# Attention inside a fused attention and MLP kernel: plain float32 products in two halves of the tensor engine, in place of products of split float32r parts

## The chip, the core and the metric

One core of one Trainium2 chip runs the whole kernel. The metric is the device time of one execution in microseconds (us), from the profiler's first to last instruction or from the timed runs. A core has a tensor engine (TensorE; PE in the rows, its weight loads PEld), a vector engine (DVE), a scalar engine (ACT), GpSimd (POOL) and a sync engine (SP), which here issues DMAs. Each works through its own list of instructions in order; semaphores tie the lists together. TensorE writes to PSUM, 8 banks of 2 KB per partition; the other engines copy from there to SBUF.

## What is computed

The kernel chains three parts. The change is in the first:

```python
batch, n_heads, seq, head_dim = (4, 12, 448, 64)
q_n, k_n = rmsnorm(q, g_q), rmsnorm(k, g_k)
scores = (1 / sqrt(head_dim)) * q_n @ k_n.T
attn = exp(scores - max(scores)); attn = attn / sum(attn)
attn_out = attn @ v                       # float32
x = attn_out as [1792 tokens, 768]
x = top-1 mixture of 8 experts (768 -> 1024 -> 768), gated
return two-layer MLP (768 -> 2048 -> 768)
```

All inputs and outputs are float32.

## The kernel before

The attention works on 24 pairs of heads (a, b of one batch). The 448 tokens of a head are three columns of 128 and a tail of 64; the two tails share one column, so a pair has seven columns a0 a1 a2 t b0 b1 b2. The schedule is written out by hand: seven slots a pair, one column a slot. In a slot TensorE does four transposes of probabilities (turn_p, L296), the scores of a column (scores, L276) and a part of the product with v (mix, L341 and L342); transposes of q and k (L229, L246) and the product that brings the result back to rows of tokens (back, L366 to L370) come between. DVE takes the row maxima (L281), ACT the exponentials (L287). Scores run ahead: turn_p is five slots behind them and mix seven.

The products of the attention use float32r, which TensorE takes in one pass, with every float32 operand split into two float32r parts, a high and a low one. Both parts of a query, 64 dimensions each, lie below each other on the 128 partitions, as weights; keys come as two tensors kh and kl. So one score column of a head is two products of 448 columns with all 128 rows of the array (all four part products). The tail column takes four, with weights padded by zeros (qm). The product with v is of the same kind: weights are the parts of v side by side (64 + 64 columns), and the probabilities are split after their transpose, into ph by ACT (L322) and pl by DVE (L330).

The splits are made by ACT (high parts: L199, L209, L248, L322) and by DVE or GpSimd (low parts: L204, L214, L253, L330). The normalized keys are doubled side by side by a DMA or a copy (kn). GpSimd also does the 1/rms by Newton's method and parts of the sums.

The product back (L366 to L370) multiplies by a matrix comb, [identity; identity] and 8 columns of the gate's weights, in plain float32. A plain float32 product is one instruction in the program and two in the trace, each with its own weights. The tails of the two heads go to the two halves of one output (L366 to partitions 0 to 63, L367 to 64 to 127), with 64 columns of weights each; these are the only products of the kernel before that stand side by side in the array.

In the first pairs some extra transposes of the identity (fill, L269) keep TensorE busy. After each batch of six pairs the routing of its tokens runs in small steps between the slots. The end of the last pair is written out by hand, together with the first transposes for the experts (L1027); the expert products start at L982. What follows does not change.

Of the kernel before, what the change touches and what calls it, by code (L numbers as in the profile page):

```python
# [8 lines left out]
F32 = mybir.dt.float32  # L9
# [7 lines left out]
E = 8  # L17
SLOTS = 1792
ND = 8
# [10 lines left out]


def attention(tc, ctx, q, k, v, const, ps, late, finish_half, tick, early):
# [8 lines left out]
    ident, identr, comb, gg = const["ident"], const["identr"], const["comb"], const["gg"]  # L41
    pool = lambda name, bufs: ctx.enter_context(tc.tile_pool(name=name, bufs=bufs))
    raw_p, spl_p, sm_p, tr_p, pp, phl, fix = (pool("raw", 2), pool("spl", 2), pool("sm", 2), pool("tr", 2), pool("pp", 2),
                                              pool("phl", 3), pool("fix", 1))
    NP = B * H // 2
    NR = 3
    qm, vm, pm = [], [], []

    def setup(*rs):
        for r in rs:  # L50
            qm.append(fix.tile([128, 2, 128], F32R, name=f"qm{r}"))
            vm.append(fix.tile([128, 2, 128], F32R, name=f"vm{r}"))
            pm.append(fix.tile([128, 576], F32, name=f"pm{r}"))
            nc.gpsimd.memset(qm[r].bitcast(F32), 0.0)
            nc.gpsimd.memset(vm[r].bitcast(F32), 0.0)
            nc.gpsimd.memset(pm[r], 0.0)
    st = [dict() for _ in range(NP)]

    # ---- per pair, before its scores
    def load(p, names):  # L60
        R = st[p]
        b, h = divmod(2 * p, H)
        for nm in names:
            src = dict(q=q, k=k, v=v)[nm]
            t = raw_p.tile([128, 8, D], F32, name="raw" + nm, tag="raw" + nm, bufs=3 if nm == "v" else 4)
            R[nm] = t[:, 0:7]
            nc.sync.dma_start(out=t.rearrange("p (i c) d -> p i (c d)", i=2)[:, :, 0:3 * D],
                              in_=src[b, h:h + 2, 0:384].rearrange("i (p c) d -> p i (c d)", c=3))
            nc.sync.dma_start(out=t[:, 3], in_=src[b, h:h + 2, 384:448])

    # 1/rms of the tokens of one or two pairs at a time
# [4 lines left out]
    fill = {0: 2, 2: 4, 4: 4, 14: 2, 16: 3}  # L76

    # what the vector engine takes from GpSimd, pair by pair, until GpSimd is ahead
    on_vector = dict(scale_k=(0, 1, 2), scale_q=(0, 2), q_low=(0,), v_low=(0,), sums=(0, 2, 3, 8), root=(0, 1))
# [4 lines left out]
    def squares(p, i):  # L84
        R, Z = st[p], sh[batch_of[p]]
        if i == 0:
            R["sq"] = raw_p.tile([128, 2, 7, D], F32, name="sq", tag="sq")
            if p == batch_of[p][0]:
                Z["ms"] = sm_p.tile([128, 2, 2, 7], F32, name="ms", tag="ms")[:, 0:len(batch_of[p])]
# [20 lines left out]
    def root(p, i=None):  # L110
        """1/rms by Newton's method, an instruction at a time; of a batch, or of k (i = 0) or q of a pair"""
# [6 lines left out]
        small = lambda name, dt=F32: sm_p.tile([128, 28], dt, name=name, tag=name)[:, 0:n]  # L118
# [33 lines left out]
        yv = y.rearrange("p (b a u o) -> p b a u o", a=2, u=7, o=1)  # L152
        rq = sm_p.tile([128, 2, 7, 1], F32, name="rq", tag="rq")[:, 0:len(bt)]
# [21 lines left out]

    def scale_k(p):
        R = st[p]
        R["kn"] = spl_p.tile([128, 7, 2, D], F32, name="kn", tag="kn")
        eng = engine("scale_k", p)
        eng.tensor_tensor(out=R["kn"][:, :, 0], in0=R["k"], in1=R["rk"].to_broadcast([128, 7, D]), op=ALU.mult)  # L180
        if p < 2:
            copy_k(p)
        elif p > 3:
            nc.sync.dma_start(out=R["kn"][:, :, 1], in_=R["kn"][:, :, 0])

    def copy_k(p):
        R = st[p]
        nc.vector.tensor_copy(out=R["kn"][:, :, 1], in_=R["kn"][:, :, 0])

    def scale_q(p):  # L190
        R = st[p]
        R["qn"] = raw_p.tile([128, 7, D], F32, name="qn", tag="qn")
        eng = engine("scale_q", p)
        eng.tensor_tensor(out=R["qn"], in0=R["q"], in1=R["rq"].to_broadcast([128, 7, D]), op=ALU.mult)

    def q_high(p):
        R = st[p]
        R["qs"] = spl_p.tile([128, 7, 2, D], F32R, name="qs", tag="qs", bufs=3)
        nc.scalar.activation(out=R["qs"][:, :, 0], in_=R["qn"], func=ACTF.Copy)  # L199

    def q_low(p):
        R = st[p]
        eng = engine("q_low", p)
        eng.tensor_tensor(out=R["qs"][:, :, 1], in0=R["qn"], in1=R["qs"][:, :, 0].bitcast(F32), op=ALU.subtract)  # L204

    def v_high(p):
        R = st[p]
        R["vs"] = spl_p.tile([128, 7, 2, D], F32R, name="vs", tag="vs", bufs=3)
        nc.scalar.activation(out=R["vs"][:, :, 0], in_=R["v"], func=ACTF.Copy)  # L209

    def v_low(p):
        R = st[p]
        eng = engine("v_low", p)
        eng.tensor_tensor(out=R["vs"][:, :, 1], in0=R["v"], in1=R["vs"][:, :, 0].bitcast(F32), op=ALU.subtract)  # L214

    def v_tail(p):
        t = st[p]["vs"][:, 3].rearrange("p a d -> p (a d)")
        for i in range(2):
            s = slice(64 * i, 64 * i + 64)
            nc.gpsimd.tensor_scalar(out=vm[p % NR][s, i], in0=t[s].bitcast(F32), scalar1=1.0, scalar2=1.0, op0=ALU.mult, op1=ALU.mult)  # L220

    def turn_q(p, i):
        R = st[p]
        if i == 0:
            R["Q"] = tr_p.tile([128, 6, 128], F32R, name="Q", tag="Q", bufs=3)
        us = (0, 1, 2, 3) if i == 0 else (4, 5, 6)
        t = ps.tile([128, 4, 128], F32R, name="tq", tag="pt" if p == 0 else "tq")
        for j, u in enumerate(us):
            nc.tensor.transpose(out=t[:, j], in_=R["qs"][:, u].rearrange("p a d -> p (a d)"), identity=identr)  # L229
        tf = t.bitcast(F32)  # L230
        nc.scalar.activation(out=R["Q"][:, 3 * i:3 * i + 3], in_=tf[:, 0:3], func=ACTF.Copy)
        if i == 0:
            m = qm[p % NR]
            nc.scalar.activation(out=m[:, 0, 0:64], in_=tf[:, 3, 0:64], func=ACTF.Copy)
            nc.scalar.activation(out=m[:, 1, 64:128], in_=tf[:, 3, 64:128], func=ACTF.Copy)

    def turn_k(p, i):
        R = st[p]
        if i == 0:
# [1406 lines left out]
```

## Time and profile before

| what | value |
|---|---|
| median of 3 timed runs | 1177.55 us (1176.89 to 1181.33) |
| span of the profiled execution (the only time given for it) | 1178.3 us |
| first score product of the attention | 16.6 us |
| last score product of the attention | 346.7 us |
| first product of the experts | 358.7 us |
| TensorE busy, whole span | 97% |
| mean granted clock of TensorE | 0.992 of full speed |

The attention takes the first 30% of the span. The span is 0.7 us above the median of the timed runs; sums below are made against the span. A share of busy time over the whole span says little on the attention; it is read from the stretches of its pairs.

### The profile page before, as it was taken

To read this page: it belongs to the slowest core of one execution; us is meant where nothing else is said; L and a number is where in the kernel's file an instruction comes from. 1 tells how busy PE (TensorE), PEld (TensorE's weight loads), DVE (VectorE), ACT (ScalarE), POOL (GpSimd) and SP (SyncE) were. 2 spreads that over 40 slices of the span, in tenths; PEclk is the share of its full clock that TensorE was granted. 3 is DMA by queue.
4 is the path that set the end of the run, shared out by engine and by line. 5 is a ranking of instruction groups with operands and counts; after the bars stand their busy time and mean duration, and the time that the engine had idled before them with its cause. 6 is when DMAs were issued, how large, how long until landed. Compare 5 with 4: busy or idle time off the path is not lost. (4 is left out here: it accounts for less than half of the span.)

```text
span 1178.3 us, 20906 instructions
## 1 busy us (share of the span) xinstructions
PE 1140.2 (97%) x7189; PEld 1009.1 (86%) x7189; DVE 879.5 (75%) x1709; ACT 732.5 (62%) x1494; POOL 409.0 (35%) x644
## 2 busy tenths in 40 slices
PE   6899999999998999999999999999999999999997
PEld 5778888888888998999999978888888888888996
DVE  7898988988977666888988978885644445444674
ACT  6889989888864566665556645553544345443664
POOL 5777676765421122255554444440200001000100
PEclk8999999999999999999999999999999999999999
DMA  4323323223036689899999923340200001000100
GB/s 113 79 64 93 113 63 106 69 64 93 17 95 186 196 283 293 264 325 284 280 301 296 297 78 107 108 129 19 108 1 1 1 14 68 1 1 1 54 1 28
DMA packets 145368, 138.25 MB, mean 117 GB/s; under 512 B 39903, under 2 KB 125919, under 8 KB 144741
## 3 DMA queue, kind: packets, MB, share of 16 engines
q1 hardware_dynamic: 141252, 120.30, 34.2%
q0 software_dynamic: 4000, 16.53, 4.0%
q8 instruction: 59, 0.97, 0.3%
q14 instruction: 57, 0.46, 0.1%
HBM read 117.26 MB, written 18.10 MB: 115 GB/s over the span
## 5 line engine op out<-in xcount | busy, mean ns | idle before, releaser
L974 DVE TENSOR_TENSOR l<-ld,h 128x768 fp32r<-128x768 f32 x159 | 151.6, 970 | 18.9 <-ACT h L969 16.3
L946 POOL TENSOR_SCALAR cva<-cva 128x384 f32<-128x384 f32 x64 | 110.3, 1724 | 144.1 <-ACT cva L945 143.8
L969 ACT ACTIVATE h<-ld 128x768 fp32r<-128x768 f32 x159 | 130.6, 840 | 9.9 <-PE hs L993 6.5
L1466 POOL DMA_INDIRECT out_dram<-ld,oidx x11 | 12.8, 1162 | 336.6 <-ACT ld L1463 212.9
L281 DVE TENSOR_REDUCE nb<-s 128x1 f32<-128x448 f32 x168 | 103.8, 618 | 22.1 <-PE s L276 20.8
L1418 ACT ACTIVATE u<-hp,half 128x512 f32<-128x512 f32 (+1 forms) x64 | 40.4, 631 | 110.2 <-PE hp L982 110.2
L330 DVE TENSOR_TENSOR pl<-pt,ph 128x448 fp32r<-128x448 f32 (+1 forms) x168 | 104.1, 620 | 4.8 <-ACT ph L322 4.7
L287 ACT ACTIVATE P<-s,nb 128x448 f32<-128x448 f32 x144 | 92.5, 642 | 22.4 <-DVE nb L281 21.7
L1425 DVE SCALAR_TENSOR_TENSOR w<-u 128x512 f32<-128x512 f32 (+1 forms) x64 | 39.9, 624 | 84.3 <-ACT u L1418 84.1
L322 ACT ACTIVATE ph<-pt 128x448 fp32r<-128x448 f32 (+1 forms) x168 | 93.4, 556 | 8.6 <-PE pt L296 7.2
L1190 ACT ACTIVATE rh<-hp 128x256 fp32r<-128x256 f32 x64 | 24.6, 384 | 107.3 <-PE hp L982 107.3
L982 PE MATMUL hp<-yh,h 128*128 128x512 f32 (+1 forms) x384 | 88.9, 368 | 2.2 <-DVEq L1369 2.2
L1016 PE MATMUL a<-l,gh 128*128 128x512 f32 x240 | 89.8, 404 | 0.0
L1016 PE MATMUL a<-h,gh 128*128 128x512 f32 x240 | 89.0, 400 | 0.0
L1016 PE MATMUL a<-h,gl 128*128 128x512 f32 x240 | 88.8, 400 | 0.0
L982 PE MATMUL hp<-yl,h 128*128 128x512 f32 (+1 forms) x384 | 87.8, 365 | 0.0
L1433 DVE TENSOR_TENSOR gl<-u,gh 128x512 fp32r<-128x512 f32 (+1 forms) x64 | 40.2, 628 | 63.6 <-ACT gh L1432 63.4
L982 PE MATMUL hp<-yh,l 128*128 128x512 f32 (+1 forms) x384 | 87.3, 363 | 0.0
L1432 ACT ACTIVATE gh<-u 128x512 fp32r<-128x512 f32 (+1 forms) x64 | 36.9, 576 | 80.8 <-PE a L1017 78.3
L296 PE MATMUL pt<-ident,P 128*128 128x128 f32 x504 | 82.4, 273 | 0.0
L982 PEld LDWEIGHTS hp<-yl,h 128*128 128x128 f32 x384 | 67.3, 190 | 11.4
L982 PEld LDWEIGHTS hp<-yh,l 128*128 128x128 f32 x384 | 66.8, 189 | 11.2
(342 smaller groups left out, 3452.8 us busy)
## 6 DMA issues: line engine op xcount, KB each, us to landing
ld<-in_moe_w_dram SPq DMA_DIRECT2D x160, 384.0 KB
raw<-in_moe_w_in_dram SPq DMA_DIRECT2D x32, 384.0 KB
ld<-in_moe_w_out_dram SPq DMA_DIRECT2D x26, 384.0 KB
rawk<-in_k_dram SPq DMA_DIRECT2D x24, 192.0 KB
rawq<-in_q_dram SPq DMA_DIRECT2D x24, 192.0 KB
rawv<-in_v_dram SPq DMA_DIRECT2D x24, 192.0 KB
xt_d<-x SPq DMA_DIRECT2D x4, 1152.0 KB
kn<-kn SPq DMA_DIRECT2D x20, 224.0 KB
```

Of the source, the lines that this page charges most:

```text
L281: nc.vector.tensor_reduce(out=R["nb"][:, u:u + 1], in_=R["s", u], op=ALU.max, axis=AX.X, negate=True)
L287: nc.scalar.activation(out=o, in_=R.pop(("s", u)), func=ACTF.Exp, bias=R["nb"][:, u:u + 1], accum_out=R["sum"][:, w:w + 1])
L296: nc.tensor.transpose(out=out, in_=src, identity=ident)
L322: nc.scalar.activation(out=R["ph", m], in_=t, func=ACTF.Copy)
L330: nc.vector.tensor_tensor(out=R["pl", m], in0=t, in1=R["ph", m].bitcast(F32), op=ALU.subtract)
L946: nc.gpsimd.tensor_scalar(out=R["a"], in0=R["a"], scalar1=2.0 ** -15, scalar2=122879.9921875, op0=ALU.max, op1=ALU.min)
L969: nc.scalar.activation(out=h, in_=src, func=ACTF.Copy)
L974: (engine or self.nc.vector).tensor_tensor(out=l, in0=src, in1=h.bitcast(F32), op=ALU.subtract)
L982: nc.tensor.matmul(out=t[:, 0:n], lhsT=w[:, k], rhs=x[:, k, 0:n], start=i == 0 and k == 0, stop=i == 2 and k == 5)
L1016: nc.tensor.matmul(out=a[j], lhsT=p[:, c], rhs=q[:, 0:512], start=first and i == 0, stop=last and i == 2)
L1418: nc.scalar.activation(out=u, in_=t[:, s], func=ACTF.Relu, scale=0.5, bias=half)
L1433: nc.vector.tensor_tensor(out=gl[:, 0:n], in0=u, in1=gh[:, 0:n].bitcast(F32), op=ALU.subtract)
```

## The change

The splits go. A score column of a head is one plain float32 product with the 64 dimensions of that head on 64 partitions: head a on partitions 0 to 63, head b on 64 to 127, so that the two heads use the upper and the lower half of the array's rows. The product with v puts head a on output partitions 0 to 63 and head b on 64 to 127 (64 columns of weights each). The tails' column uses a quarter of the array for each head.

A pair now has four units instead of seven slots, three columns with both heads and one of tails. A unit has eight transposes (five in the tails' unit), the scores of both heads into two PSUM banks, and the product with v. Head b's scores are made in two pieces of 64 and 384 columns, so that its tail keys come first. There is one row maximum for both heads (896 columns), two exponentials, and one plain copy for each head of the transposed probabilities (take_p, one by ACT, one by DVE). The schedule keeps its seven slots; units stand in the even ones, and the turning of q, of k and the product back have one even slot each. Keys are no longer doubled; q and k of four pairs stay in fixed tiles. PSUM: pt 2 banks, s 4, av 1, tq 1 (before 2 each). The fill transposes are gone, and the last pair's end is written anew.

```diff
     def scores(p, u):
         R = st[p]
-        t = ps.tile([128, S], F32, name="s", tag="s")
-        for _ in range(fill.get(7 * p + u, 0)):
-            nc.tensor.transpose(out=t[:, 0:128], in_=ident, identity=ident)
-        if u == 3:
-            ops = [(qm[p % NR][:, i], R[nm, i]) for i in range(2) for nm in ("kh", "kl")]
-        else:
-            i = u // 4
-            ops = [(R["Q"][:, u - i], R[nm, i]) for nm in ("kh", "kl")]
-        for j, (w, x) in enumerate(ops):
-            nc.tensor.matmul(out=t, lhsT=w, rhs=x, start=j == 0, stop=j == len(ops) - 1)
+        t = ps.tile([128, 2, 512], F32, name="s", tag="s", bufs=2)
+        for i, h in enumerate(halves2):
+            if u < 3:
+                o, w = t[:, i], R["Q"][h, 128 * u:128 * u + 128]
+            else:
+                o, w = t[h, 0], R["Q"][h, 384:S]
+            x = R["K"][h]
+            for d, n in ((0, S),) if i == 0 else ((384, 64), (0, 384)):
+                e = (d + 64 * i) % S
+                nc.tensor.matmul(out=o[:, e:e + n], lhsT=w, rhs=x[:, d:d + n], start=True, stop=True)
...
+    def take_p(p, m, i):
+        R = st[p]
...
+        o, t = R["PT", m][:, i, 0:S], R["pt", m][i][:, 0:S]
+        if i == 0:
+            nc.scalar.activation(out=o, in_=t, func=ACTF.Copy)
         else:
+            nc.vector.tensor_copy(out=o, in_=t)
 
     def mix(p, m):
         R = st[p]
-        for i in ((0,), (0,), (0,), (0, 1), (1,), (1,), (1,))[m]:
...
-            nc.tensor.matmul(out=R["av", i], lhsT=w, rhs=R["ph", m][:, c], start=first, stop=False)
-            nc.tensor.matmul(out=R["av", i], lhsT=w, rhs=R["pl", m][:, c], start=False, stop=last)
+        if m == 0:
+            R["av"] = ps.tile([128, S], F32, name="av", tag="av", bufs=1)
+        for i, h in enumerate(halves2):
+            if m < 3:
+                nc.tensor.matmul(out=R["av"][h], lhsT=R["v"][:, 4 * i + m], rhs=R["PT", m][:, i, 0:S], start=m == 0, stop=False)
+            else:
+
+                for d, n in ((64, 384), (0, 64)) if i == 0 else ((64, S),):
+                    e = (d - 64) % S
+                    nc.tensor.matmul(out=R["av"][h, e:e + n], lhsT=R["v"][h, 3], rhs=R["PT", m][h, 0, d:d + n], start=False, stop=i == 1 or d == 0)
...
+        t = ps.tile([128, 7, 72], F32, name="xo", tag="tq")
+        o = R["o"]
         for c in range(3):
...
+            nc.tensor.matmul(out=t[:, 2 * c:2 * c + 2], lhsT=o[:, 128 * c:128 * c + 128], rhs=comb[:, r], start=True, stop=True)
+        for i, h in enumerate(halves2):
+            nc.tensor.matmul(out=t[h, 6], lhsT=o[h, 384:S], rhs=comb[h, r, i], start=True, stop=True)
...
+    LAG = 5
+    for n in range(7 * NP):
+        t = n % 7
+        s = n // 7 * 4 + t // 2
+        if t % 2 == 0:
+            at(turn_p, s, LAG)
+            for f, a in onpe.get(n, ()):
+                f(*a)
+            at(scores, s, 0)
...
+            at(mix, s, LAG + 1)
+            at(expo, s, 1, 0)
+            at(take_p, s, LAG, 0)
+            at(take_p, s, LAG, 1)
...
+            if t == 6:
+                at(expo, s, 1, 1)
+            at(row_max, s, 0)
+        else:
+            at(expo, s, 1, 1)
```

TensorE in the kernel before, one slot in the middle of the attention (pt: transposed probabilities, s: scores, tk: transposed keys, av: the product with v):

```order
L296 MATMUL pt<-ident,pm_377 128x128
L296 MATMUL pt<-ident,P 128x128 x3
L276 MATMUL s<-kh,Q 128x448
L276 MATMUL s<-kl,Q 128x448
L246 MATMUL tk<-ident,kn 128x128 x4
L341 MATMUL av<-ph,vs 128x448
L342 MATMUL av<-pl,vs 128x448
```

Here all products use the whole array, and transposes, scores and the product with v follow each other in one form. TensorE in the changed kernel, one unit at the same place (xo: the product back; each row that is no transpose of pt is a float32 product):

```order
L247 MATMUL pt<-ident,pm_157 128x128
L247 MATMUL pt<-ident,P 128x128 x3
L247 MATMUL pt<-ident,pm_157 128x128
L247 MATMUL pt<-ident,P 128x128 x3
L314 MATMUL xo<-comb,osb 128x144 x3
L316 MATMUL xo<-comb,osb 64x72 x2
L223 MATMUL s<-K,Q 128x448
L223 MATMUL s<-K,Q 128x64
L223 MATMUL s<-K,Q 128x384
L288 MATMUL av<-pT,rawv 64x448 x2
```

Whole array (L247, L314), quarters (L316), row halves (L223) and column halves (L288) now follow each other inside every unit.

ACT in the kernel before, in the middle of the attention (sq: squares for the rms, osb: the copy of av out of PSUM):

```order
L287 ACTIVATE P,sum<-s,nb 128x448
L322 ACTIVATE ph<-pt 128x448
L94 ACTIVATE sq<-rawk 128x448
L287 ACTIVATE P,sum<-s,nb 128x448
L322 ACTIVATE ph<-pt 128x448
L94 ACTIVATE sq<-rawq 128x448
L350 ACTIVATE osb<-av 128x448
```

and in the changed kernel:

```order
L204 ACTIVATE K<-tq,gg 128x448
L239 ACTIVATE P,sum<-s,nb 128x448
L278 ACTIVATE pT<-pt 128x448
L298 ACTIVATE osb<-av 128x448
L239 ACTIVATE P,sum<-s,nb 128x448 x2
L278 ACTIVATE pT<-pt 128x448
```

An exponential (L239) now shares ACT with one copy for every two of them instead of one each, and the copies of q, v and the high parts are gone.

## Rows read from the trace of the kernel before

**Rows 1.** The page: busy time of each engine, share of the span, instructions.

```profile
PE 1140.2 (97%) x7189; PEld 1009.1 (86%) x7189; DVE 879.5 (75%) x1709; ACT 732.5 (62%) x1494; POOL 409.0 (35%) x644
```

**Rows 2.** Stretches from pair to pair: length; busy PE, PEld, DVE, ACT, POOL; clock; DMA.

```profile
16.60:28.40 11.80, 9.40 (x53) 6.42 (x51) 10.45 (x31) 9.35 (x27) 5.05 (x12) 0.90 0.55 125
...
88.10:101.00 12.90, 12.90 (x93) 11.52 (x92) 11.14 (x25) 12.51 (x33) 8.34 (x16) 1.00 0.42 106
88.10:170.00 81.90, 79.86 (x560) 69.81 (x558) 74.98 (x187) 74.64 (x194) 58.64 (x127) 1.00 0.33 89
```

**Rows 3.** Score products of the six whole columns of all pairs: durations, first and last start.

```profile
L276 PE MATMUL s<-kh,Q x144: 447/450/741, 16.6 to 346.7; 128*128 128x448 f32 x144
```

**Rows 4.** TensorE in order of time, one slot: start us, us, engine, line, what.

```profile
183.43 0.27 PE L296 MATMUL pt<-ident,pm 128*128 128x128 f32 x1
...
183.78 0.45 PE L276 MATMUL s<-kh,Q 128*128 128x448 f32 x1
184.07 0.36 PE L276 MATMUL s<-kl,Q 128*128 128x448 f32 x1
184.27 0.36 PE L341 MATMUL av<-ph,vs 128*128 128x448 f32 x1
184.68 0.38 PE L296 MATMUL pt<-ident,pm 128*128 128x128 f32 x2
```

**Rows 5.** Eight float32 passes of 128 columns, with 112 columns of weights.

```profile
340.10 1.04 PE L762 MATMUL ptab<-olg,ohi 128*112 128x128 f32 x8
340.89 0.45 PE L341 MATMUL av<-ph,vs 128*128 128x448 f32 x1
```

**Rows 6.** The tails' products side by side, last pair: weight loads, then products.

```profile
357.74 0.13 PEld L366 LDWEIGHTS xo<-comb,osb 128*64 128x64 f32 x1 [0.40 <-PE tp L1027]
357.77 0.13 PEld L367 LDWEIGHTS xo<-comb,osb 128*64 128x64 f32 x1
357.79 0.14 PEld L366 LDWEIGHTS xo<-comb,osb 128*64 128x64 f32 x1
357.83 0.14 PEld L367 LDWEIGHTS xo<-comb,osb 128*64 128x64 f32 x1
358.04 0.19 PEld L370 LDWEIGHTS xo<-comb,osb 128*128 128x128 f32 x1
...
357.85 0.23 PE L366 MATMUL xo<-comb,osb 128*64 128x72 f32 x1
357.89 0.23 PE L367 MATMUL xo<-comb,osb 128*64 128x72 f32 x1
```

**Rows 7.** TensorE before and after the tails' products of another pair.

```profile
185.43 0.37 PE L276 MATMUL s<-kl,Q 128*128 128x448 f32 x1
185.72 0.28 PE L366 MATMUL xo<-comb,osb 128*64 128x72 f32 x1
186.00 0.89 PE L370 MATMUL xo<-comb,osb 128*128 128x72 f32 x6
```

**Rows 8.** Groups of instructions, 0 to 400 us: busy us, mean ns | idle before.

```profile
L281 DVE TENSOR_REDUCE nb<-s 128x1 f32<-128x448 f32 x168 | 103.8, 618 | 22.1 <-PE s L276 20.8
L322 ACT ACTIVATE ph<-pt 128x448 fp32r<-128x448 f32 (+1 forms) x168 | 93.4, 556 | 8.6 <-PE pt L296 7.2
L287 ACT ACTIVATE P<-s,nb 128x448 f32<-128x448 f32 x144 | 92.5, 642 | 22.4 <-DVE nb L281 21.7
L287 ACT ACTIVATION_READ_ACCUMULATOR P<-s,nb 128x1 f32 x144 | 30.0, 209 | 0.0
```

**Rows 9.** The start of the first pair, in order of time.

```profile
11.33 1.13 DVE L194 TENSOR_TENSOR qn<-rawq,rq 128x448 f32<-128x448 f32 x1
...
16.64 0.74 PE L276 MATMUL s<-kh,Q 128*128 128x448 f32 x1
```

**Rows 10.** The end of the attention: last scores, first products of the experts.

```profile
346.70 0.45 PE L276 MATMUL s<-kh,Q 128*128 128x448 f32 x1
...
358.73 0.95 PE L982 MATMUL hp<-xh,e 128*128 128x256 f32 x6
```

More of the change, by code (lines that the diff above doesn't have):

```diff
@@ L206, in v_high @@
[L206 to L235, printed above, removed]
@@ new lines, in scale_k, with turn @@
+    def scale_k(p):
+        scaled(p, "kn", st[p]["k"], st[p]["rk"])
+    def scale_q(p):
+        scaled(p, "qn", st[p]["q"], st[p]["rq"])
+    def turn(p, x, name):
+        t = ps.tile([128, 512], F32, name="tq", tag="pt" if name == "Q" and p == 0 else "tq", bufs=2 if name == "Q" and p == 0 else 1)
+        for c in range(4):
+            nc.tensor.transpose(out=t[:, 128 * c:128 * c + 128], in_=x[:, 2 * c:2 * c + 2].rearrange("p i d -> p (i d)"), identity=ident)
+        st[p][name] = tr_p.tile([128, S], F32, name=name, tag=name)
+        return t[:, 0:S], st[p][name]
@@ L257, in scores, with turn_q, turn_k @@
+    def turn_q(p):
+        t, o = turn(p, st[p]["qn"], "Q")
+        nc.vector.tensor_copy(out=o, in_=t)
+    def turn_k(p):
+        t, o = turn(p, st[p]["kn"], "K")
+        nc.scalar.activation(out=o, in_=t, func=ACTF.Copy, scale=gg)
     def scores(p, u):
@@ L352, in invert, with mixed @@
+    def mixed(p):
+        R = st[p]
+        R["o"] = tr_p.tile([128, S], F32, name="osb", tag="osb")
+        nc.scalar.activation(out=R["o"], in_=R.pop("av"), func=ACTF.Copy)
     def invert(p):
@@ L393, in put @@
     def put(n, f, p, *a):
         m = place.get(p, {}).get(f.__name__, n)
-        sched.setdefault(m if type(m) is int else m[a[0]], []).append((f, (p,) + a))
+        if f is load and a == ("v",):
+            m = n
+        m = m if type(m) is int else m[a[0]]
+        (onpe if f in (turn_q, turn_k, back) and m >= 0 else sched).setdefault(m, []).append((f, (p,) + a))
     for bt in batches:
@@ L400, in attention @@
             y = z + 7 * (j - (len(bt) - 1))
-            put(y - 37, load, p, "kq")
+            put(y - 33, load, p, "kq")
             put(y - 29, squares, p, 0)
@@ L481, in begin @@
             else:
                 f(*a)
[L483 removed]
     begin()
[L485 to L502 removed]
+    N = 4 * NP
@@ L519 @@
+    turn_p(y, 3)
+    expo(z, 3, 0)
+    take(y, 3)
+    mix(y, 2)
+    turn_p(z, 0, "s")
+    mix(y, 3)
+    take(z, 0)
+    mixed(y)
+    turn_p(z, 1)
+    invert(z)
+    back(y)
+    take(z, 1)
+    mix(z, 0)
+    finish(y)
+    turn_p(z, 2, "s")
+    mix(z, 1)
+    take(z, 2)
+    turn_p(z, 3)
+    take(z, 3)
+    early(0)
+    mix(z, 2)
+    early(3)
+    mix(z, 3)
+    mixed(z)
+    early(1)
+    early(6)
+    early(4)
+    back(z)
+    finish(z)
+    early(2)
+    early(5)
 class Route:
@@ L1565, in late @@
                 else:
-                    for p in halves:
-                        nc.sync.dma_start(out=comb[p, :, 64:72], in_=wv)
+                    for i, p in enumerate(halves):
+                        nc.sync.dma_start(out=comb[p, :, i, 64:72], in_=wv[i])
                     route.load(moe_modality_id, moe_modality_bias)
```

336 lines of the change are left out of this document (121 added, 215 removed).

## The prediction

> **What bounds the kernel now.** I read the page first, then the stretches of single pairs, then TensorE in order of time. The page shows TensorE busy for 97% of the span [rows 1], which says where to look and not more, since ends of products are modelled. The stretches say it for the attention: a pair without routing takes 12.9 us, with TensorE busy for all of it, DVE for 11.1 and ACT for 12.5 at full granted clock, 1.00 or 2.4 GHz [rows 2]. So DVE and ACT have little room, but TensorE has none. Six pairs with one batch's routing take 81.9 us, 4.5 more than six times 12.9 [rows 2]. The order of time agrees: a slot of four transposes and four float32r products takes 1.25 us, from 183.43 to 184.68, and a product 0.20 (184.07 to 184.27) [rows 4]; the transposes are left with (1.25 - 4 x 0.205) / 4 = 0.11 each. Seven such slots are 8.75 us; turning q and k, the tails' extra products and the product back fill the 12.9.
>
> **Price of a float32 product.** The trace has no float32 product of 448 columns. Eight float32 passes of 128 columns take 0.79 us, 340.10 to 340.89, about 0.10 each [rows 5]; in the last pair a pass of 72 columns takes 0.06, from the weights' load at 357.79 (when the pass before it starts) to 357.85 [rows 6]. That is 0.77 to 0.83 ns a column, against 0.20/448 = 0.46 for float32r. I take 0.385 us for a pass of 448 and 0.77 for its two passes: one float32 product costs as much as almost four of float32r. The change has 16 such products a pair (four units, two heads, scores and v) in place of 32 of float32r, 32 x 0.205 = 6.6 us. Alone they would be 12.3 us; in pairs that run side by side 6.2. So on products TensorE gains next to nothing even if the halves overlap fully.
>
> **Do halves overlap?** Column halves do. The weights of L366 and L367 are loaded 0.03 us apart, the second passes' weights 0.04 apart, and the second passes start 0.04 apart, though a pass takes 0.06 [rows 6]: the two heads' passes alternate and run side by side. This carries the product with v. No product here has its rows in halves; for the scores the price lies between full overlap and none.
>
> **Price of changing the form.** From the last whole-array product at 185.43, which ends at 185.63, to the weights' load of the first half product at 185.72 pass 0.09 us in which nothing is issued [rows 7]. On the way back it is the same: the last half pass starts at 357.89 and ends 0.06 later, at 357.95; the next whole weights load at 358.04, 0.09 later [rows 6]. And the load, hidden otherwise, is now in the open: 0.055 us for 64 columns (357.74 to 357.79 [rows 6]) and about 0.11 for 128 (six passes from 186.00, each with its load, span 0.89 with the last one's 0.28 [rows 7], so 0.12 from one to the next, where 72 columns alone take 0.06). So a change costs 0.09 plus a load, and a unit has three: whole to rows, rows to columns, columns to whole; the tails of the product back add one a pair. The Trainium skill, page "TensorEngine Tiling (Array Packing)", section "Key Properties", says that a change of tiling mode drains the engine; the trace agrees with its 0.09 us for columns, and no run here shows rows. By a reading in which only tiles change and nothing drains, the sum would be the first faster rival below.
>
> **TensorE for one pair after.**
> Scores of a whole column: 0.09 + 0.11 for weights, then head b's chain: two passes of 64 columns that last as long as the next weights' load, 2 x 0.11, and two of 384, 2 x 0.33; together 1.07, three times 3.2 us. (Head a's 0.77 lies beside it.) The tails' unit: 0.09 + 0.055 + 0.77 = 0.92. The product with v: the same 0.92, four times 3.7. Back to whole: 4 x (0.09 + 0.11) = 0.8. Transposes: 29 of probabilities and 8 of q and k, 37 x 0.11 = 4.1. Product back: six passes of 144 columns, 6 x 0.12 = 0.7, and the tails 0.09 + 0.055 + 0.12 = 0.27: 1.0. Sum 13.7 us against 12.9.
>
> **Other engines.** ACT after: seven exponentials of 0.64 + 0.21, three copies of at most 0.56, and four more (two squares, K, osb) no longer than an exponential, 2.6: 10.2 us at most, since neighbouring spans overlap [rows 8]. DVE: three maxima over 896 columns at twice 0.62 or less, one of 0.62, five copies of no more than that, and small ones for finish and rms for which I allow two more: 8.7 us. Both fall well below 13.7, so the splits taken off them shorten nothing in a steady pair; they would be worth something only where TensorE waits. There are two such places. Routing costs 4.5 us a batch now; 0.8 of it are the eight passes of [rows 5], as much again I allow for its other products, and 1.1 for waits, with DVE at 8.7: I keep 2.7, about 8 us for the three batches inside the loop where 13.5 stood. And the start: the first query's normalization begins at 11.33 and takes 1.13, yet the first score waits until 16.64 for the split, a second transpose and two copies [rows 9]; without the split four transposes (0.5) and a copy (0.6) follow, so it starts at about 13.7.
>
> **The sum.** First score 13.7. Pair 0 has only scores, and DVE sets its pace: four maxima, the root of pair 1 and scales of pair 2, about 9 us (11.8 before [rows 2]). Pair 1 lacks one unit of transposes, two of v and the product back: 10. The other 22: 22 x 13.7 = 301.4. Routing 8, waits in early pairs 2. That ends the loop at 344.1, with the last score 2.0 before it, at 342.1 (346.7 now [rows 3, 10]). Behind the last score stand now 12.0 us, 346.7 to 358.7 [rows 10]; 7.6 of these are TensorE's: 21 transposes (2.3), 16 products (3.3), one and a half products back of 12 passes each (2.0). After, the lag of five units leaves 34 transposes (3.7), six units of v with their way back (6.7) and two products back (2.0), beside the 4.4 us that are not the attention's; the single tq buffer, which the experts' first transposes share with both products back, costs some 1.5 more: with the scores themselves, 0.9, the experts begin at 361.3. That is 2.6 us later than 358.7. The rest of the program is the same: 1178.3 + 2.6 = 1181 us, which is 3 us above the median of the timed runs. By its own terms (a pass 0.375 to 0.40, first pairs 4 us either way, tail 3) this case lies between 1168 and 1196.
>
> The fill transposes that are gone kept the clock up in the first pair, where it was 0.90 [rows 2]. TensorE waits there for others anyway; at 1.2 GHz pair 0 would take some 4 us more, which is inside that range.
>
> **The rivals.**
> Faster: the row halves need no drain and their weights load behind the transposes. Then every unit saves 0.09 + 0.10 on the way in, 0.75 us a pair, 18 in all: 1163. If no change of form costs anything, 13 x 0.09 and 1.1 us of loads go, 2.3 a pair, 54 in all: 1127, and then waits for ACT begin to count. For it: the trace shows no change to rows. Against it: both changes of form that it shows cost the same 0.09.
>
> Slower: row halves overlap in part. If head b's chain starts a pass behind head a's, each of the four score units is 0.385 longer, 4 x 0.385 x 24 = 37: 1218. Measured on four row tiles, the Trainium skill, page "TensorE: Matmul & The Clock Gate", section "Part 3: Packing small matmuls — row/col tiling", gives a speedup of 3.07, not 4; by that ratio alone 0.77 would be 1.0 and the time 1203, an estimate; no row here shows it. If the row halves run one after the other, or both kinds of halves by one pass in turn, a unit gains 0.77, 3.1 a pair, 74 in all: 1255. If no half overlaps, 6.2 a pair: 1329; the column halves of rows 6 speak against that.
>
> The change doing nothing because the attention is hidden can be left out: the experts' first products wait for its last rows [rows 10].
>
> **Chances.** My sum 0.43; the faster rivals 0.32 (1163: 0.21, 1127: 0.11), since rows in halves are the one form that the trace does not show, and more than half of the changes of form touch them; the slower 0.25 (1218: 0.08, 1255: 0.12, all in turn 0.05). The likeliest time is 1181. The range runs from 1140, which leaves out the case without any drain, to 1256, which leaves out the one without any overlap. A difference under 0.5%, 6 us, can't be told from no change here: of my sum 0.06 lies below 1172, 0.22 inside, 0.15 above; with the rivals faster 0.37, same 0.23, slower 0.40.
>
> **What would show it.** In the trace after: first passes of the two heads' scores some 0.01 us apart and a unit's scores in 0.9 to 1.1 us (right), or 1.6 (row halves in turn). 0.09 us of nothing before each change of form, with weights in the open; if weights of row halves load while transposes run, the first rival. Pairs of 13.7 us with ACT and DVE at about 70%. First score near 13.7, last near 342, experts near 361. The prediction is wrong if a pair is under 13 or over 15 us, or if TensorE waits for PSUM (pt, tq) inside a steady pair, which I put at nothing because DVE and ACT have 3 us to spare in each.

## The result

The changed kernel takes 1189.4 us, median of 4 runs (1186.3 to 1190.4), beside 1177.8 of the kernel before: ratio 1.009, interval 1.007 to 1.011. It is slower by 1%, 11.6 us between the medians, where 1181 was predicted. The profiled execution took 1188.6 us and its span is 1186.9; before it was 1178.3. The prediction was summed on the span: there the kernel is 8.6 us longer, where 2.6 were forecast.

The page of the kernel after, to be read beside [rows 1]:

```profile
PE 1153.1 (97%) x7126; PEld 928.4 (78%) x7126; DVE 804.8 (68%) x1465; ACT 627.4 (53%) x1229; POOL 352.7 (30%) x550
```

ACT lost 105 us of work, DVE 75, POOL 56; TensorE gained 13. The stretches answer to [rows 2]: pair 0, pair 1, a steady pair, and six pairs with one batch's routing (length, busy PE, PEld, DVE, ACT, POOL, clock, DMA share, GB/s).

```profile
12.97:26.30 13.33, 8.47 (x32) 4.90 (x33) 8.76 (x25) 5.07 (x14) 2.08 (x6) 0.62 0.59 140
26.30:46.80 20.50, 14.21 (x73) 8.52 (x73) 10.52 (x18) 11.12 (x28) 11.84 (x33) 0.83 0.11 30
88.52:101.90 13.38, 13.38 (x90) 7.86 (x89) 7.98 (x14) 8.05 (x21) 5.96 (x11) 1.00 0.33 86
88.52:171.65 83.13, 82.68 (x554) 49.33 (x553) 56.14 (x127) 48.16 (x127) 44.89 (x104) 1.00 0.26 73
```

A steady pair is 13.38 us, TensorE busy for all of it, where 12.90 stood; DVE and ACT work 8.0 us of it. Pairs 0 and 1 together take 33.8 us: TensorE is busy for 22.7 of them, part of it at the lower clock (0.62 and 0.83), and idle for 11.2. In the kernel before the two took 27.1 us, with 22.0 busy and 5.1 idle ([rows 2] for pair 0, and for pair 1):

```profile
28.40:43.70 15.30, 12.61 (x87) 10.72 (x84) 14.85 (x30) 13.80 (x37) 10.82 (x31) 1.00 0.18 48
```

TensorE in order of time in a steady pair (start, us, engine, line, what, count; a product's row ends after the next has begun, so starts are compared):

```profile
185.03 1.14 PE L223 MATMUL s<-K,Q 64*128 64x448 f32 x6
186.10 0.97 PE L288 MATMUL av<-pT,rawv 128*64 128x448 f32 x4
187.00 0.33 PE L247 MATMUL pt<-ident,pm 128*128 128x128 f32 x1
187.17 0.49 PE L247 MATMUL pt<-ident,P 128*128 128x128 f32 x3
```

The scores of a whole column take 1.07 (185.03 to 186.10), the product with v 0.90 (186.10 to 187.00), the first transpose behind it 0.17 where the others take 0.11. The change to row halves, the last transpose and then the weights' loads:

```profile
188.26 0.27 PE L194 MATMUL tq<-ident,kn 128*128 128x128 f32 x1
188.46 0.52 PEld L223 LDWEIGHTS s<-K,Q 64*128 64x128 f32 x6 [0.17 <-issue]
```

That transpose has its 0.11 until 188.37, and the first load starts at 188.46: 0.09 us in which nothing is issued.

The milestones, in us of the span, before and after: first score 16.6 and 13.0; start of pair 2 43.7 and 46.8; start of pair 23 334.2 and 336.6; last score 347.0 and 348.2 [rows 10 show the start of its first part, 346.7]; experts' first product 358.7 and 366.0; first of their second products (a) 371.0 and 382.0; end 1178.3 and 1186.9. So the 8.6 us of span come about as follows: -3.7 at the first score, +6.8 in pairs 0 and 1, -1.9 from there to the last score (pairs 2 to 4 gain 2.7, steady pairs and routing lose), +6.1 between the last score and the experts, +3.7 in the experts' first 16 us; 2.4 are regained later, and no run shows by what.

Where TensorE waits between 10 and 48 us (waiting engine, tile, line <- for whom: us, times, longest):

```profile
PE tq L194 <- DVE kn L181: 4.6, 2, 3.3
PE tq L194 <- DVE qn L181: 3.8, 2, 2.7
PE tq L194 <- POOL qn L181: 3.4, 1, 3.4
PE s L223 <- DVE Q L200: 2.4, 2, 1.6
```

Of these 14.2 us 11.8 are waits for the scaled keys and queries of the next pairs. The kernel before waits 11.5 us in the same stretch, for its keys, queries and split probabilities. And the end, in order of time:

```profile
362.88 1.00 PE L314 MATMUL xo<-comb,osb 128*128 128x144 f32 x6 [1.41 <-DVE xl L993]
...
365.22 1.09 PE L988 MATMUL tp<-ident,xg 128*128 128x128 f32 x4 [1.06 <-DVE lg L599]
365.96 1.83 PE L943 MATMUL hp<-xh,e 128*128 128x256 f32 x6
...
371.83 0.37 PE L670 MATMUL pr<-oh,tri_r 128*128 128x40 f32 x1 [2.02 <-DVE oh L642]
...
374.32 1.48 PE L943 MATMUL hp<-xl,h 128*128 128x256 f32 x6
```

The two waits of 1.41 and 1.06 are for the one tq bank; the third, 2.02, is for the routing. Behind it six products of 256 columns take 1.48 us; the same products at the full clock take 0.88. The stretches of ten microseconds show the clock, first of the kernel after, then of the one before:

```profile
360.00:370.00 10.00, 7.34 (x44) 5.98 (x44) 4.78 (x12) 3.63 (x7) 3.23 (x3) 0.83 0.39 146
370.00:380.00 10.00, 7.42 (x34) 7.37 (x35) 6.50 (x38) 2.54 (x4) 0.00 (x0) 0.59 0.64 188
380.00:390.00 10.00, 10.00 (x69) 9.44 (x69) 7.49 (x25) 3.94 (x7) 1.07 (x1) 0.90 0.54 159
```

```profile
360.00:370.00 10.00, 7.15 (x47) 6.80 (x46) 7.27 (x35) 3.07 (x5) 0.00 (x0) 0.83 1.01 318
370.00:380.00 10.00, 9.70 (x73) 8.89 (x71) 8.54 (x33) 3.94 (x7) 1.26 (x2) 1.00 0.57 166
```

So the kernel before has a stretch at the lower clock here too: by single microseconds it stands at 0.50 from 364 to 367 us, behind a wait of 1.46 for the routing. The kernel after has two, from 365 to 368 and from 372 to 382.

### The profile page after: what moved, and what is told of

Same layout as the page of the kernel before. It is cut to its first block, busy times and chain, and to the rows that moved or that the text cites. A ratio compares the mean times of both kernels' runs of the same rounds, so it can differ in the third digit from the quotient of the medians.

```text
span 1186.9 us, 19858 instructions
## 1 busy us (share of the span) xinstructions
PE 1153.1 (97%) x7126; PEld 928.4 (78%) x7126; DVE 804.8 (68%) x1465; ACT 627.4 (53%) x1229; POOL 352.7 (30%) x550
## 5 line engine op out<-in xcount | busy, mean ns | idle before, releaser
L229 DVE TENSOR_REDUCE nb<-s 128x2 f32<-128x896 f32 x72 | 78.3, 1088 | 49.0 <-PE s L223 48.9
L223 PE MATMUL s<-K,Q 64*128 64x448 f32 (+3 forms) x576 | 108.9, 468 | 2.4 <-DVE Q L200 2.4
L239 ACT ACTIVATE P<-s,nb 128x448 f32<-128x448 f32 x144 | 91.1, 635 | 36.1 <-DVE nb L229 36.0
L1151 ACT ACTIVATE rh<-hp 128x256 fp32r<-128x256 f32 x64 | 24.6, 385 | 111.7 <-PE hp L943 111.7
L247 PE MATMUL pt<-ident,P 128*128 128x128 f32 x492 | 77.9, 275 | 0.0
L943 PEld LDWEIGHTS hp<-yh,h 128*128 128x128 f32 x384 | 64.6, 191 | 13.9 <-PEq L1330 2.6
```

What stands on the lines that cost most here:

```text
L223: nc.tensor.matmul(out=o[:, e:e + n], lhsT=w, rhs=x[:, d:d + n], start=True, stop=True)
L229: nc.vector.tensor_reduce(out=R["nb"][:, 2 * u:2 * u + 2], in_=R["s", u][:, :, 0:S], op=ALU.max, axis=AX.X, negate=True)
L239: nc.scalar.activation(out=o, in_=R["s", u][:, i, 0:S], func=ACTF.Exp, bias=R["nb"][:, w:w + 1], accum_out=R["sum"][:, w:w + 1])
L247: nc.tensor.transpose(out=out, in_=src, identity=ident)
L943: nc.tensor.matmul(out=t[:, 0:n], lhsT=w[:, k], rhs=x[:, k, 0:n], start=i == 0 and k == 0, stop=i == 2 and k == 5)
```

## The experiments

All are edits of the changed kernel. Medians, ratio to the kernel before on the same chip with its interval, and from each trace the length of pairs 0 and 1 together, a steady pair, and the experts' start. The kernel before has medians from 1177.8 to 1180.9 us on these chips, so rows are best compared by their ratios:

| kernel | us | ratio | pairs 0+1 | steady | experts |
|---|---|---|---|---|---|
| after | 1189.4 | 1.009 [1.007, 1.011] | 33.8 | 13.38 | 366.0 |
| e_nob | 1175.6 (one run) | | 33.0 | 13.01 | 355.6 |
| e_rot | 1192.9 | 1.0116 [1.0095, 1.0138] | 33.3 | 13.53 | 370.6 |
| e_group | 1191.4 | 1.0107 [1.0084, 1.013] | 32.2 | 13.61 | 367.2 |
| e_fill | 1185.9 | 1.0058 [1.0037, 1.0078] | 32.0 | 13.38 | 364.9 |
| e_tail | 1184.2 | 1.0039 [1.0023, 1.0055] | 33.5 | 13.38 | 362.7 |
| e_early | 1183.3 | 1.0034 [1.0019, 1.005] | 28.9 | 13.38 | 359.1 |
| e_both | 1180.4 | 0.9992 [0.9979, 1.0006] | 27.8 | 13.38 | 357.1 |
| e_all | 1180.7 | 0.9992 [0.9977, 1.0008] | 27.1 | 13.28 | 355.6 |
| e_best | 1178.6 | 0.9988 [0.9973, 1.0002] | 28.5 | 13.38 | 356.3 |
| e_best_pf | 1178.9 | 0.9995 [0.9979, 1.0011] | 27.5 | 13.38 | 355.3 |
| e_best_rot | 1174.6 | 0.9958 [0.9934, 0.9982] | 27.6 | 13.19 | 351.1 |
| e_last | 1170.3 | 0.994 [0.9916, 0.9963] | 24.6 | 13.19 | 348.1 |

**e_nob: do row halves run side by side?** Head b's scores of the three whole columns are left out; maxima and exponentials read head a's instead.

```diff
-        for i, h in enumerate(halves2):
+        for i, h in enumerate(halves2[0:1] if u < 3 else halves2):
```

> Head b's scores of the three whole columns are left out (its maxima and exponentials read head a's scores instead, so the values are not those of the reference). If the two row halves run side by side, only head b's longer chain goes (two 64-column pieces, about 0.1 us a unit): a score unit goes from 1.07 us to 0.97, 72 units, 7 us less in all. If the halves run in turn, each of these units loses a whole product of 0.77 us or more: 55 us less.

The unit of scores, now two passes of head a alone:

```profile
192.41 1.02 PE L223 MATMUL s<-K,Q 64*128 64x448 f32 x2
193.35 0.60 PE L288 MATMUL av<-pT,rawv 128*64 128x448 f32 x2
```

It takes 0.94 us (192.41 to 193.35) in place of 1.07. All of head b's work was worth 0.12 us a unit, 0.37 a pair; two passes of 448 columns in turn would be worth 0.75 a unit. So the row halves run side by side, and the 0.12 is what head b's chain is longer, not its work. The time of its one run fell by 13.8 us, more than the 9 of the pairs: the clock between 370 and 380 us was 1.00 in this run.

**e_rot: head b's scores in one product.** Head b's keys are turned round in the copy out of PSUM, by three instructions of ScalarE (ACT in the rows), so that its product needs no two pieces.

```diff
-        nc.scalar.activation(out=o, in_=t, func=ACTF.Copy, scale=gg)
+        a, b = halves2
+        nc.scalar.activation(out=o[a], in_=t[a], func=ACTF.Copy, scale=gg[a])
+        nc.scalar.activation(out=o[b, 64:S], in_=t[b, 0:384], func=ACTF.Copy, scale=gg[b])
+        nc.scalar.activation(out=o[b, 0:64], in_=t[b, 384:S], func=ACTF.Copy, scale=gg[b])
...
-            for d, n in ((0, S),) if i == 0 else ((384, 64), (0, 384)):
...
+            nc.tensor.matmul(out=o[:, 0:S], lhsT=w, rhs=x, start=True, stop=True)
```

> The rotation of head b's keys moves from the score products (two pieces of 64 and 384 columns) into the copy of the keys out of PSUM (three ACT instructions instead of one), so head b's scores are one product of 448 columns. Theory that a chain of weight loads and passes in each half sets a unit's length: each of three units a pair 0.1 us shorter, about 7 us less in all, 1182. Rival, that the halves share something and only the sum of columns counts: no change, 1189, since the columns are the same.

A miss: the pair became 13.53. TensorE, then ScalarE in the same stretch:

```profile
191.21 1.02 PE L224 MATMUL s<-K,Q 64*128 64x448 f32 x4
192.17 0.98 PE L294 MATMUL av<-pT,rawv 64*64 64x384 f32 x6
...
193.24 0.49 PE L248 MATMUL pt<-ident,P 128*128 128x128 f32 x3
193.98 0.33 PE L248 MATMUL pt<-ident,pm 128*128 128x128 f32 x1 [0.25 <-ACT pT L279]
```

```profile
191.32 0.63 ACT L205 ACTIVATE K<-tq,gg 64x448 f32<-64x448 f32 x1 [3.44 <-PE tq L194]
191.96 0.58 ACT L206 ACTIVATE K<-tq,gg 64x384 f32<-64x384 f32 x1
192.44 0.30 ACT L207 ACTIVATE K<-tq,gg 64x64 f32<-64x64 f32 x1
...
193.39 0.53 ACT L279 ACTIVATE pT<-pt 128x448 f32<-128x448 f32 x1
```

The unit did fall, to 0.96, three times 0.11 a pair. But the three copies take 1.44 us (191.32 to 192.76) where one took 0.53, the copy of the probabilities behind them comes late, and the transposes that need its bank begin 0.74 behind the ones before (193.24 to 193.98) instead of 0.33. With what the transposes behind it lose too that is about 0.48 a pair lost for 0.33 won. ScalarE is busy 60% of a pair and yet cannot take 0.9 us more at this place.

**e_group: fewer changes of form.** The products with v of two units stand together in every second unit.

```diff
-            at(mix, s, LAG + 1)
+            if s % 2 == 0:
+                at(mix, s, LAG + 1)
...
+            if s % 2 == 0:
+                at(mix, s, LAG)
```

> The products with v of two neighbouring units follow each other, after the scores of every second unit. That takes away one change of form in six, two a pair, and adds nothing. Theory that each change costs 0.09 us and an open weight load of 0.055: 0.29 us a pair, 7 us less in all, 1182, with a pair of 13.1 us. Rival, that the loss against the kernel before lies in the start and the end of the attention and not in the changes of form: 1189, pair 13.4. If the second product waits for its copy of the probabilities, slower.

A miss in the sum, 13.61 us a pair, with both parts legible:

```profile
190.77 0.49 PE L247 MATMUL pt<-ident,P 128*128 128x128 f32 x3
191.38 0.14 PEld L247 LDWEIGHTS pt<-ident,pm 128*128 128x128 f32 x1 [0.36 <-ACT pT L278]
...
194.09 1.72 PE L288 MATMUL av<-pT,rawv 128*64 128x448 f32 x8
195.75 0.33 PE L247 MATMUL pt<-ident,pm 128*128 128x128 f32 x1
```

Two products with v in a row take 1.66 (194.09 to 195.75), where two apart take 1.80: one change of form with its load is worth 0.14 us, what the prediction had (0.09 + 0.055). Of the two places in a pair only this one gains, since at the other the pair of products is one of columns and one of quarters, a change again. And a unit without products with v gives the copies too little time: the transposes at 191.38, whose weights' load waits for ACT's copy, start 0.61 behind those at 190.77, instead of 0.33. The whole of that unit is 0.38 longer than its parts were, for 0.14 gained.

**e_fill: the clock at the start.** 58 transposes of the identity at the start instead of 40, and 20 and 10 before units 2 and 4.

```diff
+            if fill.get(s):
+                w = ps.tile([128, 512], F32, name="pt", tag="pt", bufs=2)
+                for _ in range(fill[s]):
+                    nc.tensor.transpose(out=w[:, 0:128], in_=ident, identity=ident)
```

> 58 transposes of the identity ahead of the attention instead of 40, and 20 and 10 more in the first pair's waits, so that TensorE's granted clock does not stand at 0.5 in the first pair. Theory that the half clock costs part of the 33.8 us that the first two pairs take: four score units of 1.7 us become 0.9, 2 to 4 us less, 1186. Rival, that the first pairs wait for the chain of 1/rms and scaling alone: the granted clock rises, the time stays at 1189.

The granted clock of the first 30 us rose from 0.83 to 0.94 and the median fell by 3.5 us, to 1185.9; the intervals of the two ratios overlap. Pairs 0 and 1 are only 1.8 shorter and pair 2 is 1.0 longer; in the trace the last score comes 1.1 earlier and the span is 0.9 shorter. So the lower clock sets little of what the first pairs take.

**e_tail: two banks for the experts' first transposes.**

```diff
-            moe.m.ps, moe.m.turn_tag = ps, "tq"
+            moe.m.ps, moe.m.turn_tag = ps, "pt"
```

> The experts' first three groups of transposes (line 988) go to the two banks of pt and no longer share the one bank of tq with the last pair's product back. In the changed kernel the tensor engine waits 1.41 us there for the subtraction of line 993 and 1.06 us for the logits of line 599. Theory (the single bank costs 2.5 us, and the pauses draw the lower clock after it): the experts' first product starts at about 363.5 instead of 366.0, the granted clock of 370 to 390 is nearer to 1.00 than 0.59 and 0.90, and the time is 1184 to 1187 (-2.5 to -5). Rival (the copies of line 992 and 993 on ScalarE and VectorE are the bound, the bank is not): start at 365 to 366, time 1188 to 1190.

```profile
361.08 1.00 PE L314 MATMUL xo<-comb,osb 128*128 128x144 f32 x6
...
362.28 0.66 PE L988 MATMUL tp<-ident,xg 128*128 128x128 f32 x4
362.69 0.72 PE L943 MATMUL hp<-xh,e 128*128 128x256 f32 x4
```

Both waits are gone. The experts begin at 362.7, 15.0 us behind the last score instead of 17.8; the clock of 370 to 380 is 0.83 instead of 0.59 and then 1.00; the median is 5.2 us less, the ratio 1.0039 where it was 1.009. On the bank the theory holds and the rival does not. The wait for the routing stays, 2.09 us, and behind it the clock is 0.50 from 371 to 373 us.

**e_early: the first pairs' steps where their inputs are ready.** The 1/rms of pair 1 runs on GpSimd, its keys and queries are both turned in slot 6 (the queries in a bank of pt), and pair 2 is scaled and turned later. The loads of pair 6 were left in slot 8 here, in e_both and in e_all, ahead of pair 2's scaling and into the same buffer, so in these three pair 2 is computed from pair 6's keys and queries; what they show is the schedule.

```diff
-    on_vector = dict(..., root=(0, 1))
+    on_vector = dict(..., root=(0,))
-    place = {1: dict(scale_k=2, scale_q=3, turn_k=4, turn_q=6),
-             2: dict(..., scale_k=7, scale_q=7, turn_q=9, turn_k=11),
+    place = {1: dict(scale_k=2, scale_q=3, turn_k=6, turn_q=6),
+             2: dict(..., scale_k=9, scale_q=9, turn_k=11, turn_q=13),
```

> The first four pairs' steps are placed later or on another engine: the 1/rms of pair 1 on GpSimd, both turns of pair 1 in slot 6 (its queries in a bank of pt), pair 2 scaled in slot 9 and turned in slots 11 and 13. Theory (pairs 0 and 1 take 33.8 us instead of 19 because the tensor engine's queue reaches turns whose inputs are not scaled yet): pairs 0 and 1 together 22 to 26 us, the time 1178 to 1182. Rival (the chain of 1/rms itself, from the loads on, is what is late, wherever the turns stand): 31 to 34 us, the time within 2 us of 1189.

Pairs 0 and 1 take 28.9 us: a gain of 4.9, the experts begin at 359.1, and the time is 1183.3. That is about half of what was expected of pairs 0 and 1, and more than the rival allowed; the time is 1.3 above the theory's range. What TensorE still waits for, 10 to 60 us:

```profile
PE tq L194 <- DVE kn L181: 3.3, 2, 1.7
PE s L223 <- ACT P L239: 2.0, 2, 1.6
PE tq L194 <- POOL qn L181: 2.0, 2, 1.4
```

**e_both and e_all.**

> e_tail and e_early together, with the transposes that fill time at the start (58, and 20 and 10 between the first units). If the parts are independent and as expected of each: 1174 to 1180; the granted clock up to 30 us over 0.9. If the early chain is bound by the loads and the 1/rms: 1182 to 1185.

1180.4: 9.0 under the changed kernel, and even with the kernel before (0.9992). The clock of the first 30 us is 1.00.

> e_both, and head b's score product in one product of 448 columns, by a copy of K with its columns turned round in place: two pieces on ScalarE and head a's piece on VectorE (in e_rot ScalarE made all three, 1.44 us in place of 0.53, and its copy of the probabilities came 0.42 us late for the tensor engine). Theory: the score unit is 0.96 instead of 1.07 and nothing waits, a steady pair 13.05 instead of 13.38, so 7 us under e_both. Rival (ScalarE is still late, or VectorE is now): a steady pair 13.3 to 13.6, and e_all not under e_both.

A miss again: 13.28 a pair. Head a's piece on VectorE (DVE in the rows) waited for ScalarE's pieces of the same tile, and ScalarE's copy of the probabilities was still late, 17 times, 4.4 us in 230.

**e_best and e_best_pf.** Pair 2 is scaled in slot 8 and pair 6 loaded in slot 10.

> As e_both, which had one slip: there the scaling of pair 2 in slot 9 came behind the load of pair 6 into the same buffer (slot 8), so pair 2 was computed from pair 6's keys and queries, and its scaling waited for that load until 29.26 us. Here pair 2 is scaled in slot 8 and pair 6 loaded in slot 10; the 1/rms of pairs 3 and 4 begins in slot 10; the fill between units stands where the tensor engine still waited (20 before unit 2, 10 before unit 3, 8 before unit 6). Theory (the order of the first pairs' steps is what is late): pairs 0 to 2 together 38 to 41 us where e_both took 42.7, and 1176 to 1179. Rival (the lower clock after the pauses takes it back, or the end does): 1180 to 1182, as e_both.

1178.6, as the theory's range had it, but pairs 0 to 2 took 41.9, not 38 to 41; the experts begin 0.8 earlier than in e_both, and the clock of 360 to 370 us is 0.83 where it was 0.66.

```diff
+        pt = self.ps.tile([128, 512], F32, name="pf", tag=self.ps_tag)
+        pf = pt[0:64, 0:E]
         nc.tensor.matmul(out=pf, lhsT=self.fold, rhs=ls[:, 6], start=True, stop=True)
+        for _ in range(18 if last else 0):
+            nc.tensor.transpose(out=pt[:, 128:256], in_=self.ident, identity=self.ident)
```

> e_best, and 18 transposes of the identity behind the product pf of the last batch's routing (line 620), where the tensor engine waits 2.09 us for VectorE's oh (line 642) and the next 7 us of products run at half the clock (six products of 256 columns 1.48 us instead of 0.88). Theory (the pause draws the lower clock): the products behind it run at 0.88, the time falls by 3 to 4 us against e_best. Rival (the lower clock comes from the thinner work of 357 to 362 before it, or at random): the same time as e_best within 1.5 us, or up to 1 us more if the transposes hold the products up.

First the same six products in e_best, then in e_best_pf with VectorE's copy of pf:

```profile
364.23 1.48 PE L948 MATMUL hp<-xl,h 128*128 128x256 f32 x6
```

```profile
361.90 0.16 DVE L633 COPY lgs<-pf 64x8 f32<-64x8 f32 x1 [1.40 <-PE pf L628]
...
364.66 0.87 PE L951 MATMUL hp<-xl,h 128*128 128x256 f32 x6
```

With 18 transposes in the pause (1.46 us of it stay idle) the products behind it run at the full clock. But the copy of pf waited 1.40 us for the transposes in its bank, and the routing's product pr came 8.1 us behind the experts' start instead of 6.6: no gain in time.

**e_best_rot: the rotation at the price of a fifth product in the turn.** The keys' turn writes the tail's 64 columns at both ends of the bank, one copy of 512 columns takes all.

```diff
+            for c in (3, 0, 1, 2):
+                n = 64 + 128 * c if c < 3 else 0
+                nc.tensor.transpose(out=t[:, n:n + 128], in_=pair(c), identity=ident)
+            nc.tensor.matmul(out=t[:, 448:512], lhsT=pair(3), rhs=ident[:, 0:64], start=True, stop=True)
...
+            nc.tensor.matmul(out=o[:, 0:S], lhsT=w, rhs=x[:, 64 - 64 * i:512 - 64 * i], start=True, stop=True)
```

> e_best_pf, and head b's scores in one product of 448 columns without the three copies of e_rot: the turn of the keys writes the tail's 64 columns at both ends of the bank (one float32 product of 64 columns by the identity more), one copy of 512 columns takes all, and head a reads columns 64 to 511, head b 0 to 447. Theory: the score unit 0.96 instead of 1.07 three times a pair, 0.12 to 0.15 more for the turn, ScalarE's copy 0.06 longer, so a steady pair 13.38 becomes 13.15 to 13.2 and the time falls 4 to 5 us against e_best_pf, to 1169 to 1174, under both kernels. Rival (something else of the pair takes it, as ScalarE did in e_rot): a steady pair over 13.3.

```profile
192.08 1.02 PE L229 MATMUL s<-K,Q 64*128 64x448 f32 x4
193.03 0.98 PE L299 MATMUL av<-pT,rawv 64*64 64x384 f32 x4
```

Both heads' scores now take 0.95, as long as head a's alone in e_nob (0.94): the overlap is whole. A steady pair is 13.19, nothing in it waits, and 1174.6 us is 4.3 under e_best_pf and under the kernel before (0.9958). One fill, kept from e_best, stood in its way, the 8 transposes before unit 6:

```profile
31.35 1.97 PE L433 MATMUL pt<-ident 128*128 128x128 f32 x8 [3.12 <-DVE pT L286]
33.11 1.06 PE L197 MATMUL tq<-ident,kn 128*128 128x128 f32 x4
```

**e_last.** That fill goes, and the one behind pf, 12 transposes now, gets a bank of its own.

> e_best_rot with two fills set right. The 8 transposes before unit 6 are gone: in e_best_rot they waited 3.12 us for VectorE's copy of a bank of pt, and the turn of pair 2's keys, ready since 25.85 us, stood behind them until 33.11. And the transposes behind pf, 12 now, go to a bank of their own: in e_best_pf VectorE's copy of pf (line 623) waited 1.40 us for the 18 in its bank, which ate what the higher clock gave. Theory: pair 1 takes 14.5 to 16 us instead of 17.47, the products behind pr run at 0.88 with pr 2.1 us behind pf, and the time is 2 to 4 us under e_best_rot (1170.5 to 1172.5). Rival (the copies of the probabilities at the end of pair 1 are the bound, whatever stands before them): pair 1 still 17 us, time 1173 to 1175.

```profile
27.72 0.49 PE L253 MATMUL pt<-ident,P 128*128 128x128 f32 x3
28.05 0.60 PE L197 MATMUL tq<-ident,kn 128*128 128x128 f32 x4
...
352.25 0.28 PE L631 MATMUL pf<-ls,fold 128*64 128x8 f32 x2
353.25 2.82 PE L635 MATMUL wf<-ident 128*128 128x128 f32 x12 [0.72 <-DVE rl L1170]
355.73 0.38 PE L685 MATMUL pr<-oh,tri_r 128*128 128x40 f32 x1
```

Pair 1 falls from 17.47 to 14.48 us and the time to 1170.3, the best of all, 0.994 of the kernel before; its interval overlaps that of e_best_rot. The second half of the theory missed: the bank came free 0.72 us after pf, the clock had fallen by then, the transposes took 2.48 us (353.25 to 355.73) and pr stood 3.5 us behind pf, not 2.1. From the experts' start to their first product a it is 14.0 us, as in e_best_rot (14.1). Of the 4.9 us that its span is shorter 3.0 are gained in pair 1 and none here; what gains the rest, behind the first product a, is not shown.

## Why the prediction was right and where it was not

The reason was right: TensorE bounds a steady pair, and side by side float32 products buy nothing. The direction was right too, but only just forecast: the sum had 2.6 us, less than the 6 us that it called too small to tell from no change, and gave slower a chance of 0.40. A pass of 448 columns, taken as 0.385, is 0.37 (e_nob's unit of 0.94, less 0.2 for the change and the load, in two). The heads run side by side in columns and rows, fully (e_nob, e_best_rot). A change of form costs its 0.09 with the load in the open, to row halves too (188.37 to 188.46); e_group shows 0.14 for one to column halves. By that the rule of the Trainium skill, page "TensorEngine Tiling (Array Packing)", section "Key Properties", that a change of tiling mode drains the engine, agrees with the trace for rows as for columns. The faster rivals, in which such changes cost nothing, are out; so are the slower ones, in which the halves take turns. The Trainium skill, page "TensorE: Matmul & The Clock Gate", section "Part 3: Packing small matmuls — row/col tiling", gives a speedup of 3.07 with four row tiles. No run here has four; with two next to nothing is lost, 0.95 us with both heads and 0.94 with one.

The steady pair was summed to 13.7 and is 13.38: scores 1.07 (1.07) and 0.91 (0.92), product with v 0.90 (0.92). Most of the difference is the way back to whole, where the load in the open was taken as 0.11 and is 0.06 (the first transpose at 187.00 takes 0.17, the others 0.11). Routing adds 2.85 us to six pairs (83.13 - 6 x 13.38), predicted 2.7. ACT and DVE have their room, 8.0 of 13.38, and no wait for PSUM in a steady pair. e_rot and e_group show how little that average says: the room is not where a late copy needs it.

The step that failed is the one on the first two pairs: "about 9 us" and "10" for pairs 0 and 1, with 2 for waits. They take 33.8. The mechanism was named, DVE and the scaling of the next pairs set the pace, but it was sized as DVE's own work in pair 0. TensorE takes its list in order: a turn whose input is not scaled yet holds up all scores, transposes and products behind it, and it waits 14 us there [the waits above]. The chain to that input got no shorter. GpSimd's steps of the 1/rms of pair 2 take 3.6 us in both kernels, those of pairs 3 and 4 take 3.8 before and 3.9 after, and the keys of pair 3 are scaled from 43.74 us before and from 44.12 after. GpSimd itself is not what holds them in the kernel after: it stands idle ahead of both until DVE's first step of the same chain is done:

```profile
25.71 0.21 POOL L135 TENSOR_TENSOR t<-y 128x16 f32<-128x16 f32 x1 [6.75 <-DVE y L126]
...
40.08 0.24 POOL L135 TENSOR_TENSOR t<-y 128x32 f32<-128x32 f32 x1 [6.51 <-DVE y L126]
```

Before, the same waits are 0.53 and 0.54 us, so where DVE's steps stand in its list has a part in it. e_early, which moves steps, one 1/rms to GpSimd and one turn to another bank, gives 4.9 back; e_last, with fills and the new turn of the keys besides, 9.2. How the rest divides between the chain's own length and the order stays open.

The fill transposes at the start were put at some 4 us in pair 0, inside the range: with e_fill pair 0 is 0.1 shorter and pair 1 is 1.7, and only the median, not the trace, falls by 3.5.

At the end, from the last score to the experts, 19.2 us were forecast and 17.8 taken, of it 2.5 for the one tq bank (forecast 1.5); e_tail takes these away. Not foreseen was the granted clock after it: "The rest of the program is the same" left out that pauses of TensorE around the experts' start are followed by a stretch at 0.59, 3.7 us, of which 2.4 come back later. e_tail shortens it together with its waits, e_best_pf shows it go when most of one pause is filled. That the length of that one pause decides is not shown: in e_early a wait of 1.46 us for the routing is followed by some 10 us at 0.50, in e_best_pf a wait of 1.46 by none.

On the span the sum missed by 6.0 us, and that is a balance of larger misses: 12.8 too little for pairs 0 and 1 (33.8 against 21 with the waits), 6.0 too much from pair 2 to the last score (301.4 against 307.4, the steady pairs being 0.3 shorter each than summed), 0.7 too much for the first score and 1.4 for the hand-over, 1.3 too little behind it. So it is in part luck that the time came so near. For the same reason it proves little that e_both, with start and end mended, takes 1180.4: pairs 0 and 1 still take 27.8 us in it.

## What to carry to other kernels

Compare columns times passes and not instructions: a plain float32 product in half an array costs what the split into float32r parts cost, and each change of form adds 0.14 to 0.2 us. A kernel in steady state is easily summed; look for the difference where it is not steady, at the first pairs and at the hand-over, and follow there what stands at the head of TensorE's list, which it works through in order. Busy shares of 60% on ScalarE do not mean that a copy can be 0.9 us longer: ask who waits for the next one.

## What the hardware showed that was not expected

- Splitting a float32 product has a price of its own: with head b's scores split 64 + 384 a unit takes 1.07, in one product of 448 it takes 0.95, as long as one head alone. In the trace after, the weights of head b's passes are loaded 0.11 us apart, where a pass of 64 columns would take 0.05.
- A wait of about 2 us at TensorE for the routing was followed by some 3 to 10 us at 0.50 of the clock (six products of 256 columns 1.48 instead of 0.87); with 18 transposes of the identity in the pause the clock stayed at 1.00, and writing them into a bank that another engine was to read delayed that engine by 1.40 us.
